# First steps of the second batch: last transposed weights ahead of the softmax, means of w1's last quarter in place of unread products

## The chip, the cores and the metric

The kernel runs on one core of a Trainium2 chip. The time is device microseconds of one execution, the median of several runs. TensorE (PE in the profile), VectorE (DVE), ScalarE (ACT), GpSimd (POOL) and the DMA queues each work through an instruction stream of their own and wait for each other by semaphores.

## The reference

Attention with a threshold is followed by a Fourier mix and a two-layer network, all in float32 (8 batches, 8 heads, 576 rows, 64 columns a head; hidden size 2048):

```python
scores = scale * q @ k.T
thresh = max(scores) - tau                       # along the row
attn = where(scores >= thresh, exp(scores - max(scores)), 0)
attn = attn / (sum(attn) + 1e-9)
x = heads side by side of (attn @ v)             # (8, 576, 512)
mixed = real(fft(fft(x, axis=1), axis=2))
u = x + mixed
un = (u - mean(u)) / sqrt(var(u) + 1e-6)         # along the row
out = u + relu(un @ w_ch1) @ w_ch2
```

The mean of a row is not taken from u. Instead each column of w_ch1 (w1 in the kernel) has its mean over the 512 input rows subtracted once, which gives the same product. For that, TensorE multiplies a quarter of w1 (512 of its 2048 columns) with a matrix of 1/512 ("means of w1"). Two of the four row blocks of w1 are also mirrored by a product with a permutation.

## The kernel before: what the change and the prediction touch

A step `i` is one tile of 128 query rows of one pair of heads; a batch has 20 steps. In a step the scores of the tile are made, then its softmax, and then the transposition of the weights of the step before, `i - 1`. Steps 20 to 39 are `second_batch`. Beside attention it does the Fourier mix of the first batch (`mix`), the last conversions of w_ch2 (`advance`: the input is float64 as integers, made float32 in several passes of VectorE, ScalarE and GpSimd), and the first products of the network (`fill`).

```python
def busy(n):                      # products that nobody reads
    for _ in range(n):
        pd = ps.tile([128, 4, 128], FP32, tag="mm", bufs=4, name="pd")
        nc.tensor.matmul(pd[:, :, :], ones[:, :], four, start=True, stop=True)   # 128x512
...
def column_means(g):              # means of w1's quarter g
    pm = ps.tile([128, 512], FP32, tag="mm", bufs=4, name="pm")
    for c in range(ND):           # 4 row blocks
        nc.tensor.matmul(pm[:, :], ones[:, :], w1[c][:, cols], start=(c == 0), stop=(c == ND - 1))
def mirrored(g):
    for c in (1, 3):
        pr = ps.tile([128, 512], FP32, tag="mm", bufs=4, name="pr")
        nc.tensor.matmul(pr[:, :], mirror[:, :], w1[c][:, cols], start=True, stop=True)
def less_mean(eng, g, c):         # L377
    rows = prs[g][c // 2][:, :] if c % 2 else w1[c][:, cols]
    eng.tensor_tensor(out=w1[c][:, cols], in0=rows, in1=means[g][:, :], op=ALU.subtract)
def copy_mean(g):                 # L1247: ScalarE, out of the product's bank
    nc.scalar.copy(mean[:, :], means[g][:, :])
...
def softmax(i, between=None, meanwhile=None):
    for j in range(nh):           # two heads
        nc.vector.tensor_reduce(out=neg[...], in_=sc[j][...], op=ALU.max, negate=True)   # L461
    meanwhile()                   # here: advance of the step before
    for j in range(nh):
        nc.scalar.activation(out=ej, in_=sc[j][...], func=ACT.Exp, bias=neg[...])        # L469
        ... thr by ScalarE (j == 0, L473)
        nc.vector.scalar_tensor_tensor(out=ej, in0=sc[j][...], scalar=thr[...], in1=ej,
            op0=ALU.is_ge, op1=ALU.mult, accum_out=den[...])                             # L477
    nc.vector.reciprocal(den, den)
    rec = ...                     # a copy by GpSimd (L501)

def weights_in_parts(i):          # transposed_weights(i) runs it to its end
    nc.tensor.transpose(pe[:, 0, :], e[:, 512:640], ident)   # L541
    nc.tensor.transpose(pe[:, 1, :], rec, ident)             # L544
    ... 4 (last tile of a pair) or 8 transposes into pw      # L560
    nc.scalar.copy(...)           # ends, recs (L548, L552), e_t (L562, L564)
def weighted_values(n, part):     # pv: 20 products (L589) of e_t and ends with v, x by VectorE (L597)
...
def first_sums_w1():              # called at the second group of tokens, about 386 us
    for c in range(2):            # L880
        nc.vector.tensor_tensor(out=s_u[c], in0=a_w1[1][0][c], in1=a_w1[1][1][c], op=ALU.add)
    for c in range(2):            # L884
        nc.vector.tensor_tensor(out=a_w1[1][0][c], in0=a_w1[0][0][c], in1=a_w1[1][0][c], op=ALU.subtract)
...
def second_batch(i):
    first = i - per_batch         # 0 to 19
    if first != 1:
        scores(i)
    softmax(i, None, lambda: (advance(first - 1), advance(first - 1)))
    ...
    if first == 0:
        transposed_weights(i - 1)
        weighted_values(n - 1, 1)
        scores(i + 1)
        busy(4)
        ... fold of x by VectorE, start of the mix
        mix(3)
        mix(3)                    # py: products of the mix (L692)
    elif first == 1:
        mix(3)
        transposed_weights(i - 1)
        busy(2)
        mix(2)                    # pa: L709, L713; then tmp (L728, L729) and u_t (L731, L735)
        advance(first)            # L298, L301, L306, L309, L312
        advance(first)
    elif first == 2:
        mix(2)
        transposed_weights(i - 1)
        mix(2)
        column_means(LAST)
        copy_mean(LAST)
        mirrored(LAST)
        for c, eng in ((1, nc.vector), (3, nc.vector), (0, nc.gpsimd), (2, nc.gpsimd)):
            less_mean(eng, LAST, c)
        weighted_values(n, 0)
        advance(first)
        advance(first)
    else:
        fill()                    # ph: hidden products (L822), relu (L827 ScalarE, L829 VectorE)
        transposed_weights(i - 1)
        ...
        if t == 3:
            prep_pair(n + 1)      # pq, pk, pt: q and k of the next pair transposed
```

Products go to PSUM tiles of one pool ("mm", four banks) and free them when their reader is done. The first two batches are written in a fixed order on all engines. From the third on only TensorE's order is fixed, and a scheduler places the other engines' instructions. It may hoist them into the earlier part: `first_sums_w1` is written there, and before the change its two sums L880 run at 170.7 and 172.5 us.

Of the kernel before, what the change touches and what calls it, by code (L numbers as in the profile page):

```python
# [47 lines left out]
def kernel(  # L48
# [12 lines left out]
    nc = tc.nc  # L61
# [43 lines left out]
    def busy(n):  # L105

        for _ in range(n):
            pd = ps.tile([128, 4, 128], FP32, tag="mm", bufs=4, name="pd")
            four = bass.AP(
                tensor=ones.tensor, offset=ones.offset, ap=[list(ones.ap[0]), [0, 4], [1, 128]]  # L110
            )
            nc.tensor.matmul(pd[:, :, :], ones[:, :], four, start=True, stop=True)  # L112
# [244 lines left out]
    def column_means(g):  # L357
        cols = slice(WC * g, WC * (g + 1))
        pm = ps.tile([128, 512], FP32, tag="mm", bufs=4, name="pm")
        for c in range(ND):  # L360
            nc.tensor.matmul(
                pm[:, :], ones[:, :], w1[c][:, cols], start=(c == 0), stop=(c == ND - 1)
            )
        means[g] = pm
# [9 lines left out]
    def less_mean(eng, g, c):  # L374
        cols = slice(WC * g, WC * (g + 1))
        rows = prs[g][c // 2][:, :] if c % 2 else w1[c][:, cols]
        eng.tensor_tensor(out=w1[c][:, cols], in0=rows, in1=means[g][:, :], op=ALU.subtract)  # L377
# [45 lines left out]
    def scores(i):  # L423
        n, t = divmod(i, NT)
        qT, kT = heads[n][0:2]

        nh = 2 if t < 4 else 1
        sc = [ps.tile([128, 2, 512], FP32, tag="sc", name=f"sc{j}") for j in range(nh)]
        if t < 4:
            for c in range(2):  # L430
                for j in range(2):
                    hp = slice(64 * j, 64 * j + 64)
                    nc.tensor.matmul(  # L433
                        sc[j][:, c, 0:HALF], qT[hp, 128 * t : 128 * t + 128],
                        kT[hp, HALF * c : HALF * (c + 1)], start=True, stop=True,
                    )
        else:

            for j, c, c0, k0, w in (
                (0, 0, 0, 0, HALF), (1, 0, 0, 64, HALF), (0, 1, 0, HALF, HALF),  # L440
                (1, 1, 0, 64 + HALF, 512 - HALF), (1, 1, 512 - HALF, 0, 64),
            ):
                hp = slice(64 * j, 64 * j + 64)
                nc.tensor.matmul(  # L444
                    sc[0][hp, c, c0 : c0 + w], qT[hp, 512:S], kT[hp, k0 : k0 + w],
                    start=True, stop=True, skip_group_check=True,
                )
        steps[i] = (sc, nh)

    def softmax(i, between=None, meanwhile=None):  # L450

        t = i % NT
        sc, nh = steps[i]
        neg = sb.tile([128, 2], FP32, tag="neg", bufs=3, name="neg")
        thr = sb.tile([128, 2], FP32, tag="thr", bufs=3, name="thr")
        den = sb.tile([128, 2], FP32, tag="den", bufs=3, name="den")


        e = sb.tile([128, 2 * S], FP32, tag="e", name="e")
        for j in range(nh):  # L460
            nc.vector.tensor_reduce(  # L461
                out=neg[:, j : j + 1], in_=sc[j][:, :, 0:HALF], axis=AXIS_XY, op=ALU.max,
                negate=True,
            )
        if meanwhile is not None:
            meanwhile()
        for j in range(nh):
            ej = e[:, S * j : S * (j + 1)].rearrange("p (c n) -> p c n", c=2)
            nc.scalar.activation(  # L469
                out=ej, in_=sc[j][:, :, 0:HALF], func=ACT.Exp, bias=neg[:, j : j + 1], scale=1.0  # L470
            )
            if j == 0:
                nc.scalar.activation(  # L473
                    out=thr[:, 0:nh], in_=neg[:, 0:nh], func=ACT.Identity,
                    bias=thr_off[:, :], scale=-1.0,
                )
            nc.vector.scalar_tensor_tensor(  # L477
                out=ej, in0=sc[j][:, :, 0:HALF], scalar=thr[:, j : j + 1], in1=ej,
                op0=ALU.is_ge, op1=ALU.mult, accum_out=den[:, j : j + 1],
            )  # L480

            nc.vector.tensor_scalar(
                out=den[:, j : j + 1], in0=den[:, j : j + 1], scalar1=1e-9, scalar2=None,
                op0=ALU.add,
            )
            if between is not None:
                between()
                between = None
        nc.vector.reciprocal(den[:, 0:nh], den[:, 0:nh])  # L489
        rec = None  # L490
        if normalized(i // NT):
            nc.vector.tensor_scalar(  # L492
                out=e[:, 0:S], in0=e[:, 0:S], scalar1=den[:, 0:1], scalar2=None, op0=ALU.mult
            )
            if nh == 2:
                nc.scalar.activation(  # L496
                    out=e[:, S : 2 * S], in_=e[:, S : 2 * S], func=ACT.Copy, scale=den[:, 1:2]
                )
        else:
            rec = sb.tile([128, 2 * D], FP32, tag="rec", name="rec")  # L500
            nc.gpsimd.tensor_copy(  # L501
                rec[:, :].rearrange("p (j d) -> p j d", j=nh), _repeated(den[:, 0:nh], 2 * D // nh)
            )
        if t == 4:
            nc.scalar.copy(e[:, S : S + 64], e[:, 512:S])
        steps[i] = (e, rec)

    def transposed_weights(i):
        for _ in weights_in_parts(i):
            pass  # L510
# [366 lines left out]

    def first_sums_w1():
        for c in range(2):
            nc.vector.tensor_tensor(  # L880
                out=s_u[c], in0=a_w1[1][0][c], in1=a_w1[1][1][c], op=ALU.add
            )
        for c in range(2):
            nc.vector.tensor_tensor(  # L884
                out=a_w1[1][0][c], in0=a_w1[0][0][c], in1=a_w1[1][0][c], op=ALU.subtract
            )
# [358 lines left out]
    def copy_mean(g):  # L1245
        mean = sb.tile([128, WC], FP32, tag="u", bufs=2, name="mean")
        nc.scalar.copy(mean[:, :], means[g][:, :])  # L1247
        means[g] = mean
# [30 lines left out]
    def advance(at):  # L1279
        for run in chunks.get(at, ()):  # L1280
            next(run, None)
# [24 lines left out]
    def mix(count):  # L1306
        nonlocal spent, mixed
        for _ in range(count):
            done = next(mixes[0], None)
            if done is None:  # L1310
                mixes.pop(0)
                mixed += 1
                break
            spent += done

    def second_batch(i):

        nonlocal budget
        n, t = divmod(i, NT)
        first = i - per_batch  # L1320
        if first != 1:
            scores(i)
        softmax(i, None, lambda: (advance(first - 1), advance(first - 1)))
        chunks.pop(first - 1, None)
        transfers(first)
        fold_more()
        if first == 0:
            transposed_weights(i - 1)
            weighted_values(n - 1, 1)
            scores(i + 1)  # L1330
            busy(4)
            folds.append(fold_rows(n - 1))
            while folds:
                fold_more()
            load_v(n + 1)
            start_batch(0)
            mix(3)
            mix(3)
        elif first == 1:
            mix(3)  # L1340
            transposed_weights(i - 1)
            busy(2)
            mix(2)
            advance(first)
            advance(first)
        elif first == 2:
            mix(2)
            transposed_weights(i - 1)
            mix(2)
            column_means(LAST)  # L1350
            copy_mean(LAST)
            mirrored(LAST)
            for c, eng in ((1, nc.vector), (3, nc.vector), (0, nc.gpsimd), (2, nc.gpsimd)):
                less_mean(eng, LAST, c)
            weighted_values(n, 0)
            advance(first)
            advance(first)
        else:
            fill()
# [3 lines that stand above are left out]
            fill()  # L1363
            if t == 3:
                prep_pair(n + 1)
            fill()
            if t == 2:
                weighted_values(n, 0)
            if t == 0:
                weighted_values(n - 1, 1)  # L1370
                folds.append(fold_rows(n - 1))
                load_v(n + 1)
        if first == 16:
            fold_halves(1)
        if first < 3:
            budget += 3 * per_slot
# [94 lines left out]
```

## Time and profile before

| what | value |
|---|---|
| time, median of 3 runs | 1679.7 us (1679.39 to 1679.97) |
| span of the profiled execution | 1678.0 us |
| TensorE, VectorE, ScalarE, GpSimd busy | 97%, 68%, 50%, 35% |
| shares of the chain that ended last | TensorE 76%, VectorE 15%, ScalarE 7% |
| mean granted TensorE clock | 0.996 of full |
| first step of the second batch (its scores) | 130.9 us |
| scores of its fourth step | 170.9 us |

An L with a number is a line of the kernel. A row of a timeline has the start and the length in us, the engine, the line, the output and inputs by the program's names, the shape and the count; in brackets stands how long the engine had been idle and what released it. A matmul in float32 leaves two records, so four products of 128x512 are x8. The chain of waits follows the work that ended last back through what released each step. Ends of matmuls are modelled; starts are better to go by.

### The profile page before, as it was taken

The numbers are of one execution on the slowest core, as the hardware profiler recorded it, in microseconds if no ns is written. First come the engines' busy times: TensorE is split into PE (matmuls) and PEld (weight loads), VectorE is DVE, ScalarE is ACT, GpSimd is POOL, SyncE is SP. The second block draws the span as 40 slices with busy tenths as digits, with TensorE's granted clock in tenths as the row PEclk, the third lists the DMA queues.
The fourth block names the chain that finished last, engine by engine and source line by source line (L and its number), as shares of the span: only waits on it lengthen the run. The fifth ranks groups of instructions, "written<-read, shape, count | busy, mean of one in ns | idle before, by whom it ended". The sixth has DMA issues, their size and how long they took to land.

```text
span 1678.0 us, 28904 instructions
## 1 busy us (share of the span) xinstructions
PE 1626.3 (97%) x10838; PEld 1277.1 (76%) x10838; DVE 1142.1 (68%) x2518; ACT 837.2 (50%) x1817; POOL 581.2 (35%) x779
## 2 busy tenths in 40 slices
PE   8998889999999999999999999999999999999998
PEld 4555555566887788878888778787878788889998
DVE  6885786565857676866576758686686858664454
ACT  5764675543545464545354546455646545432111
POOL 5773463040520433134322143213242144224232
PEclk9999999999999999999999999999999999999999
DMA  5323231010010101000101010110101010000000
GB/s 163 114 55 109 57 87 45 25 35 21 16 37 13 35 16 42 22 28 8 28 16 41 9 35 15 42 22 25 25 16 41 22 28 9 14 1 13 14 13 13
DMA packets 130384, 57.48 MB, mean 34 GB/s; under 512 B 121123, under 2 KB 121125, under 8 KB 130246
## 3 DMA queue, kind: packets, MB, share of 16 engines
q1 hardware_dynamic: 128854, 55.35, 12.3%
q8 instruction: 86, 1.41, 0.4%
q14 instruction: 52, 0.43, 0.1%
q10 hardware_dynamic: 1392, 0.30, 0.1%
HBM read 46.02 MB, written 9.44 MB: 33 GB/s over the span
## 4 chain that ended last, share of the span: by engine, by line
PE 76%; DVE 15%; ACT 7%; issue 2%; POOL 1%; DVEq 0%; ACTq 0%
PE ph L926 24%; PE po L1090 18%; PE pv L589 8%; PE sc L433 7%; PE pw L560 5%; PE po L848 3%; DVE e L477 3%; DVE neg L461 2%; ACT e L469 2%; DVE hs L1051 2%; PE sc L444 2%; PE ph L822 1%; PE py L692 1%; PE pd L112 1%; PE pa L709 1%
## 5 line engine op out<-in xcount | busy, mean ns | idle before, releaser
L469 ACT ACTIVATE e<-sc,neg 128x576 f32<-128x576 f32 x288 | 212.2, 737 | 239.5 <-DVE neg L461 238.9
L461 DVE TENSOR_REDUCE neg<-sc 128x1 f32<-128x576 f32 x288 | 206.2, 750 | 172.7 <-PE sc L433 160.9
L477 DVE SCALAR_TENSOR_TENSOR e<-sc,thr,e 128x576 f32<-128x576 f32 x288 | 229.8, 811 | 56.8 <-ACT thr L473 53.0
L1090 PE MATMUL po<-w,hs 128*128 128x256 f32 x1024 | 246.2, 383 | 0.0
L1090 PEld LDWEIGHTS po<-w,hs 128*128 128x128 f32 x1024 | 186.0, 190 | 32.8 <-issue 11.2
L926 PE MATMUL ph<-u_t,w 128*128 128x128 f32 x1536 | 187.8, 276 | 0.0
L926 PEld LDWEIGHTS ph<-u_t,w 128*128 128x128 f32 x1536 | 179.3, 192 | 4.4 <-issue 3.3
L560 PE MATMUL pw<-ident,e 128*128 128x128 f32 x1152 | 169.9, 274 | 10.5 <-ACT kT L406 2.7
L562 ACT COPY e_t<-pw 128x512 f32<-128x512 f32 x256 | 148.6, 594 | 59.9 <-PE pw L560 59.3
L433 PE MATMUL sc<-kT,qT 64*128 64x288 f32 x1024 | 167.4, 429 | 8.2 <-DVE e L477 7.6
L560 PEld LDWEIGHTS pw<-ident,e 128*128 128x128 f32 x1152 | 134.5, 141 | 29.4 <-issue 4.3
L935 DVE TENSOR_TENSOR hs<-ph,hs 128x512 f32<-128x512 f32 x160 | 107.0, 685 | 72.1 <-PE ph L926 46.8
L433 PEld LDWEIGHTS sc<-kT,qT 64*128 64x128 f32 x1024 | 92.6, 186 | 69.2 <-issue 38.8
L926 PE MATMUL ph<-t_u,s_w 128*128 128x128 f32 x1024 | 126.9, 278 | 2.1 <-POOL t_u L900 1.8
L804 DVE SCALAR_TENSOR_TENSOR u<-po,rstd,u 128x256 f32<-128x256 f32 (+1 forms) x164 | 75.5, 484 | 73.8 <-PE po L1090 71.9
L926 PEld LDWEIGHTS ph<-t_u,s_w 128*128 128x128 f32 x1024 | 120.3, 193 | 5.0 <-issue 2.3
L1090 PE MATMUL po<-hs,s_tile 128*128 128x256 f32 x512 | 122.1, 382 | 0.0
L496 ACT ACTIVATE e<-e,den 128x576 f32<-128x576 f32 x96 | 74.9, 780 | 63.6 <-DVE den L489 62.9
L1090 PEld LDWEIGHTS po<-hs,s_tile 128*128 128x128 f32 x512 | 93.6, 190 | 13.6 <-issue 2.1
L943 ACT ACTIVATE hs<-hs 128x512 f32<-128x512 f32 x112 | 69.3, 630 | 63.4 <-DVE hs L935 63.4
L622 POOL TENSOR_TENSOR half<-x 128x287 f32<-128x287 f32 x48 | 40.2, 857 | 126.5 <-ACT x L595 70.7
L492 DVE TENSOR_SCALAR e<-e,den 128x576 f32<-128x576 f32 x120 | 79.7, 664 | 3.5
(199 smaller groups left out, 2868.9 us busy)
## 6 DMA issues: line engine op xcount, KB each, us to landing
hs<-in_moe_w_ch_dram SPq DMA_DIRECT2D x23, 512.0 KB, 4.4
out_dram<-u SPq DMA_DIRECT2D x36, 256.0 KB, 2.2
qk_in<-in_q_dram SPq DMA_DIRECT2D x64, 128.0 KB, 2.4
v_in<-in_v_dram SPq DMA_DIRECT2D x64, 128.0 KB, 2.4
qk_in<-in_k_dram SPq DMA_DIRECT2D x31, 128.0 KB, 2.4
w<-in_moe_w_ch_dram SPq DMA_DIRECT2D x6, 512.0 KB, 8.3
qk_in<-in_k_dram SPq DMA_DIRECT2D x31, 64.0 KB, 2.3
stage<-in_moe_w_ch_dram SPq DMA_DIRECT2D x3, 512.0 KB, 3.9
```

The costliest lines, as they stand in the source:

```text
L433: nc.tensor.matmul(sc[j][:, c, 0:HALF], qT[hp, 128 * t : 128 * t + 128], kT[hp, HALF * c : HALF * (c + 1)], start=True, stop=True,)
L461: nc.vector.tensor_reduce(out=neg[:, j : j + 1], in_=sc[j][:, :, 0:HALF], axis=AXIS_XY, op=ALU.max, negate=True,)
L469: nc.scalar.activation(out=ej, in_=sc[j][:, :, 0:HALF], func=ACT.Exp, bias=neg[:, j : j + 1], scale=1.0)
L477: nc.vector.scalar_tensor_tensor(out=ej, in0=sc[j][:, :, 0:HALF], scalar=thr[:, j : j + 1], in1=ej, op0=ALU.is_ge, op1=ALU.mult, accum_out ...
L492: nc.vector.tensor_scalar(out=e[:, 0:S], in0=e[:, 0:S], scalar1=den[:, 0:1], scalar2=None, op0=ALU.mult)
L560: nc.tensor.transpose(pw[:, c, :], e[:, c0 : c0 + 128], ident[:, :])
L562: nc.scalar.copy(e_t[:, 4 * j : 4 * j + 4, qs], pw[:, :, :])
L589: nc.tensor.matmul(pv[64 * j : 64 * j + 64, 0:m], vt[:, 2 * c + j, :], e_t[:, 4 * j + c, 0:m] if c < 4 else ends[:, 0:m], start=(c == 0), ...
L804: nc.vector.scalar_tensor_tensor(out=u, in0=product, scalar=self.rstd[:, t : t + 1], in1=u, op0=ALU.mult, op1=ALU.add,)
L926: nc.tensor.matmul(banks[name][:, 128 * q : 128 * q + 128], left[c][:, 512 * part + 128 * q : 512 * part + 128 * q + 128], right[c], start ...
L935: nc.vector.tensor_tensor(out=to, in0=bank, in1=to if other is None else other, op=ALU.add)
L1090: nc.tensor.matmul(bank[:, 0 : DM // 2], left[p], right[p], start=start and p == 0, stop=p == NK - 1, skip_group_check=True,)
```

## The change

In the first step of the second batch (`first == 0`) the transposition of the last weights, with its copies by ScalarE, is written ahead of the softmax. Unread products that only kept TensorE at work (`busy(4)`, `busy(2)`) give way to the means and the mirrored blocks of w1's last quarter, which stood in the third step. The subtractions of the means go to the second step with them. The two sums L880 are kept in their place in the program's order, so that the scheduler no longer hoists them between the subtractions. What is computed stays the same; six unread products are gone.

```diff
     def first_sums_w1():
         for c in range(2):
-            nc.vector.tensor_tensor(
+            tc.keep_in_program_order(nc.vector.tensor_tensor(
                 out=s_u[c], in0=a_w1[1][0][c], in1=a_w1[1][1][c], op=ALU.add
-            )
+            ))
...
             scores(i)
+        if first == 0:
+
+            transposed_weights(i - 1)
         softmax(i, None, lambda: (advance(first - 1), advance(first - 1)))
...
         if first == 0:
-            transposed_weights(i - 1)
             weighted_values(n - 1, 1)
             scores(i + 1)
-            busy(4)
+            column_means(LAST)
+            copy_mean(LAST)
...
             mix(3)
             transposed_weights(i - 1)
-            busy(2)
             mix(2)
+            mirrored(LAST)
+            for c, eng in ((1, nc.vector), (3, nc.vector), (0, nc.gpsimd), (2, nc.gpsimd)):
+                less_mean(eng, LAST, c)
...
             mix(2)
-            column_means(LAST)
-            copy_mean(LAST)
-            mirrored(LAST)
-            for c, eng in ((1, nc.vector), (3, nc.vector), (0, nc.gpsimd), (2, nc.gpsimd)):
-                less_mean(eng, LAST, c)
             weighted_values(n, 0)
```

In the built program TensorE's order is otherwise the same to the end. On VectorE the two sums L880 now stand ahead of the two subtractions L884, where before only L884 stood, and some ten rows around them change places.

## The prediction

> **What bounds the kernel now.** I read the page first: its first two parts say which engine fills the span, and where in it that engine has air.
>
> ```profile
> PE 1626.3 (97%) x10838; PEld 1277.1 (76%) x10838; DVE 1142.1 (68%) x2518; ACT 837.2 (50%) x1817; POOL 581.2 (35%) x779
> PE   8998889999999999999999999999999999999998
> ```
>
> TensorE is busy 97% of 1678.0 us; the air is in the first six slices, about 250 us. The change touches TensorE between 132 and 173 us, so I asked for the busy time of each stretch there, and of a late one for comparison. After the stretch and its length come the busy time (and records) of each engine, the granted TensorE clock, and the DMA share and rate.
>
> ```profile
> 160.00:180.00 20.00, 16.23 (x81) 9.27 (x82) 13.89 (x31) 8.96 (x22) 12.74 (x14) 1.00 0.01 1
> 360.00:400.00 40.00, 40.00 (x269) 29.31 (x266) 28.63 (x66) 20.05 (x45) 7.74 (x14) 1.00 0.12 30
> ```
>
> From 360 us TensorE is full: work moved there is hidden if it is not TensorE's. At 160 us it is not full, so a wait removed there may bring time. The timeline of TensorE (start, length, what; in brackets the idle time before, and its releaser) has the pieces concerned:
>
> ```profile
> 132.30 0.60 PE L560 MATMUL pw<-ident,e 128*128 128x128 f32 x4
> 135.93 4.04 PE L589 MATMUL pv<-e_t,v_in 128*64 128x320 f32 x16 [3.03 <-ACT e_t L564]
> ...
> 163.24 3.70 PE L361 MATMUL pm<-w,ones 128*128 128x512 f32 x8
> 166.78 1.88 PE L371 MATMUL pr<-w,mirror 128*128 128x512 f32 x4
> ...
> 178.11 0.65 PE L398 MATMUL pq<-ident,qk_in 128*128 128x128 f32 x4 [2.10 <-ACT hs L827]
> ```
>
> The product pv waits 3.03 us for ScalarE's copy e_t. ScalarE's timeline says why: the copies stand behind the two exponentials of the next tile, though what they copy was finished at 132.9.
>
> ```profile
> 132.92 0.74 ACT L469 ACTIVATE e<-sc,neg 128x576 f32<-128x576 f32 x1 [1.32 <-DVE neg L461]
> ...
> 134.41 0.41 ACT L552 COPY ends<-pe 64x64 f32<-64x64 f32 x2
> 134.84 0.42 ACT L552 COPY recs<-pe 64x64 f32<-64x64 f32 x2
> 135.29 0.58 ACT L564 COPY e_t<-pw 128x512 f32<-128x512 f32 x1
> ```
>
> After that idle time TensorE's clock drops: single microseconds of the same table give 0.50 until 139.2.
>
> ```profile
> 136.00:137.00 1.00, 1.00 (x4) 0.46 (x6) 0.12 (x1) 0.00 (x0) 0.29 (x1) 0.50 0.66 250
> 138.00:139.00 1.00, 1.00 (x6) 0.47 (x4) 0.00 (x0) 0.00 (x0) 0.00 (x0) 0.50 1.12 397
> ```
>
> Lastly VectorE from 165 to 175 us, where its order holds up the softmax that TensorE waits for at 178.11:
>
> ```profile
> 167.91 0.69 DVE L377 TENSOR_TENSOR w<-pr,mean 128x512 f32<-128x512 f32 x1 [3.09 <-PE pr L371]
> 170.65 1.22 DVE L880 TENSOR_TENSOR s_w<-w,w 128x1024 f32<-128x1024 f32 x1 [2.05 <-POOL w L377]
> 171.79 0.68 DVE L377 TENSOR_TENSOR w<-pr,mean 128x512 f32<-128x512 f32 x1
> 172.51 1.23 DVE L880 TENSOR_TENSOR s_w<-w,w 128x1024 f32<-128x1024 f32 x1
> 173.65 0.42 DVE L597 TENSOR_TENSOR x_first<-pv,recs 128x256 f32<-128x256 f32 x1
> ```
>
> Two waits (3.09 and 2.05 us) and two sums of 1.2 us stand ahead of x_first, and the chain of waits runs through exactly these rows: POOL w L377 to 170.6, s_w, w, s_w, x_first, then L298 and ScalarE to pq.
>
> [...] s_w waits 2.05 us, with a ready subtraction behind it. [...] a second drop (mean clock 0.73 in 234 to 236 us) follows 2.53 us of idle. [...] L298 takes 0.89 us beside a busy GpSimd (156.7) and 0.42 us beside an idle one (174.0).
>
> **The change part by part.** I take the starts of before and carry a shift along the chain; minus is earlier.
>
> 1. *Copies ahead of the exponentials.* TensorE's order here is unchanged; ScalarE's is turned round. The rows pe are done at about 132.45. The four small copies and e_t take 1.37 us in a row (134.51 to 135.88 in the chain), so e_t ends at about 133.9 and pv starts at about 133.95 instead of 135.93: **-2.0**. Idle before it falls from 3.03 to about 1.05 us.
> 2. *The clock.* In before the 20 products of pv take 4.63 us (135.93 to 140.56); the same 20 take about 2.9 us at full clock (192.72 to 195.6, twin of this group). With 1.05 us of idle I expect no drop: **-1.7**. pv then ends at about 136.9. The exponentials now start at 133.9 rather than 132.92, and VectorE's softmax ends at about 137.05 rather than 136.1; that is 0.15 behind pv's end and becomes the limit for x. The shift there is about **-3.55**.
> 3. *Means for busy(4).* Four products of 128x512 replace four of 128x512: 3.58 us (141.60 to 145.3) against 3.54 (163.24 to 166.78). Both lie beside VectorE's fold, whose first result lets py start at 145.44. Zero; the shift stays -3.55. The copy of the mean (0.58) falls into 10.9 us of ScalarE's idle time before 146.77.
> 4. *busy(2) gone, mirrored in.* The first pa starts at 153.93 after 1.79 us of unread products; its inputs are done by 151.9 and the products before it at 152.1. So pa moves by -5.35. The two mirrored products (1.8 us) come behind pa and ahead of the next scores, which move by -3.75. VectorE does two subtractions of 0.65 us more before L298, but pa reached it 1.8 us sooner: L298 moves from 156.82 to about 153.0, **-3.8**. GpSimd's two subtractions (2.5 us) follow four additions that start 5.35 us earlier. They end at about 156.9, where L319 (160.54 before) is due at 156.75: 0.15 lost or nothing.
> 5. *The place they left.* pm and pr took 5.35 us of TensorE (163.24 to 168.59) between the last pa and pv. Now pv follows pa at about 159.45: **-9.2** for pv, the scores after it, and the first hidden product. GpSimd's additions to u_t, which that product's third matmul needs, end near 164.3, when it is due: no loss.
> 6. *VectorE without subtractions and sums.* x_first had waited for all four rows until 173.74. Now it waits only for pv's end, about 161.75, so it starts near 161.85: -11.9. GpSimd is still busy until 164.3, so L298 and L301 may take 1.6 us instead of 0.7, giving back about 1.0. The softmax, ScalarE's relu L827 and pq at 178.11 then move by **-10.9**. The first hidden product ends at about 165.7, so it is not the bound, and the 2.10 us idle ahead of pq nearly closes.
> 7. *The sums later.* In the built order they stand beside the two subtractions L884, which ran at 386.1 to 388.6. They need 2 x 1.2 us of VectorE, in a stretch where TensorE has no idle time. The softmax's den and normalization move back by about 3.2 us. The weights they feed would be ready at about 394.6, and TensorE asks at 395.94: no loss, at most +0.5.
>
> From 180 us on the order is the same on all engines but for this spot, and transfers are issued relative to the computation. The shift should reach the end whole: -10.9 and up to +0.5. I take -10.6: 1679.7 - 10.6 = 1669.1.
>
> **The rivals.**
> (a) *The clock stays half speed behind pv.* [...] Against: 1.69 us before 161.58 and 2.10 us before 178.11 drew no drop in the trace. It would leave -9, 1670.5.
> (b) *GpSimd becomes the bound.* Its additions to u_t, the subtractions of w1 and the conversion stand in one queue from 151 to 164 us, and the hidden product waits for the last of them. If GpSimd runs 2 us later than I have it, the hidden product and ScalarE's relu follow: -9, 1670.7. For it: my two figures meet at 164.3 without slack. Against: VectorE's softmax is about 1.2 us behind anyway.
> (c) *The early gain is swallowed later.* From 360 us TensorE is full, and full TensorE absorbs nothing: work only starts sooner. A transfer could catch it, but the seven weight transfers issued at 134 to 138 us are on the way until about 147, and the first use moves to 153. I give it little. It would make 1674 to 1679.
> (d) *Fewer unread products cool the clock elsewhere*[...]: 1.6 us either way.
>
> **Range and chances.** -10.6 is the sum; (a) and (b) each cost about 2, (d) is plus or minus 1.6, and part 6 may bring 1 more[...]. So 1666 to 1673 in 8 of 10 cases. Faster by 2% would need 33.6 us, three times all that is at stake: 0.005. Slower by 2% would need something broken in the later schedule: 0.01.
>
> **What would show it.** Right: pv starts near 134 with about 1 us of idle, its 20 products take about 2.9 us at clock 1.00, pa starts near 148.6, the second scores after it near 161.8, and pq near 167.2. Wrong: a clock of 0.50 anywhere from 134 to 168; TensorE idle ahead of the first hidden product with a GpSimd u_t row as releaser (b); new idle time of TensorE from 386 to 400 us (part 7); or a shift that is -10 at 180 us and smaller at 400 (c).

## The result and the profile after

The changed kernel takes 1668.51 us (median of 4 runs, 1668.08 to 1671.41) against 1679.55 us: ratio 0.9938, 95% interval 0.9921 to 0.9955. A second series gave 1668.99 us and 0.9936 (0.9923 to 0.9948). That is 11 us, 0.6%.

The profiled execution was the slowest of the four (1671.41 us); its span is 1669.6 us. Up to the first step's scores it runs 1.36 us later than the profile of before, because TensorE's clock fell once more, for 3.41 us from 17.9 us on. I therefore measure each kernel from its own first scores of the second batch (130.86 us in before, 132.22 here).

The page shows the engine lines hardly changed; TensorE's busy time fell by 4.5 us, and one of the first slices is a tenth fuller.

```profile
PE 1621.8 (97%) x10826; PEld 1273.6 (76%) x10826; DVE 1146.0 (69%) x2518; ACT 837.9 (50%) x1817; POOL 581.9 (35%) x779
PE   8998899999999999999999999999999999999998
```

TensorE's timeline of the changed kernel, the pieces that answer to those of before (start, length, what; in brackets the idle time before and its releaser):

```profile
133.66 0.60 PE L560 MATMUL pw<-ident,e 128*128 128x128 f32 x4
135.40 2.37 PE L589 MATMUL pv<-e_t,v_in 128*64 128x320 f32 x16 [1.14 <-ACT e_t L564]
...
151.74 1.88 PE L371 MATMUL pr<-w,mirror 128*128 128x512 f32 x4
...
164.12 1.56 PE L822 MATMUL ph<-u_t,w 128*128 128x384 f32 x4
167.35 1.56 PE L822 MATMUL ph<-u_t,w 128*128 128x384 f32 x4 [1.67 <-POOL u_t L735]
...
169.84 0.60 PE L398 MATMUL pq<-ident,qk_in 128*128 128x128 f32 x4
```

The wait ahead of pv is 1.14 instead of 3.03 us, and its first 16 records take 2.37 instead of 4.04 us. (A product leaves two records: what the prediction calls the 20 products of pv are 10 products in 20 records.) The 2.10 us ahead of pq are gone. In their place stands a new wait: the hidden product ph stops in its middle for 1.67 us, for GpSimd's last row of u_t. Single stretches of the table of busy times have the clock under pv at 1.00:

```profile
134.00:136.00 2.00, 0.86 (x9) 0.38 (x9) 0.91 (x2) 1.93 (x7) 0.00 (x0) 1.00 0.27 60
136.00:138.00 2.00, 2.00 (x18) 0.99 (x14) 1.69 (x5) 0.80 (x2) 0.00 (x0) 1.00 0.56 108
```

ScalarE's copies now stand ahead of the exponential:

```profile
133.86 0.42 ACT L552 COPY ends<-pe 64x64 f32<-64x64 f32 x2 [0.90 <-PE pe L544]
...
134.76 0.59 ACT L564 COPY e_t<-pw 128x512 f32<-128x512 f32 x1
135.24 0.75 ACT L469 ACTIVATE e<-sc,neg 128x576 f32<-128x576 f32 x1
```

VectorE's timeline, where x_first now waits for nothing but pv:

```profile
152.80 0.69 DVE L377 TENSOR_TENSOR w<-pr,mean 128x512 f32<-128x512 f32 x1
153.66 0.69 DVE L377 TENSOR_TENSOR w<-pr,mean 128x512 f32<-128x512 f32 x1 [0.17 <-PE pr L371]
...
157.13 1.66 DVE L314 SCALAR_TENSOR_TENSOR w<-hs,w 128x512 f32<-128x512 uint32 x1
...
163.14 0.42 DVE L597 TENSOR_TENSOR x_first<-pv,recs 128x256 f32<-128x256 f32 x1 [0.74 <-PE pv L589]
```

One row is to be kept in mind: L314 took 1.66 us. The same row of before took 0.68 us. In the changed kernel GpSimd's two subtractions stand beside it. VectorE's timeline of before, then GpSimd's of the changed kernel:

```profile
159.72 0.68 DVE L314 SCALAR_TENSOR_TENSOR w<-hs,w 128x512 f32<-128x512 uint32 x1
```

```profile
155.55 2.69 POOL L377 TENSOR_TENSOR w<-w,mean 128x512 f32<-128x512 f32 x2
158.93 1.27 POOL L319 TENSOR_TENSOR w<-w,hs 128x512 f32<-128x512 f32 x1 [0.69 <-ACT tmp L724]
...
163.66 0.88 POOL L731 TENSOR_TENSOR u_t<-x,tmp 1x289 f32<-1x289 f32 x1
...
166.08 1.22 POOL L735 TENSOR_TENSOR u_t<-x,tmp 1x287 f32<-1x287 f32 x1
```

L314 ends at 158.79 us, 0.55 us after the second subtraction (158.24).

**Where the gain arises, and that it stays.** The table has, for each kernel, how much sooner the scores of the second to fifth step start than in before, each counted from the first step's scores (starts in TensorE's timeline; before: 9.57, 24.96, 40.04 and 51.32 us after them). The runs below are in it too.

| kernel | 2nd | 3rd | 4th | 5th | median us | ratio (95%) |
|---|---|---|---|---|---|---|
| predicted | -3.55 | -3.75 | -9.2 | -10.9 | 1669.1 | |
| changed, first profile | -3.55 | -3.63 | -9.31 | -9.91 | 1668.51 | 0.9938 (0.9921 to 0.9955) |
| changed, again | -3.55 | -3.62 | -9.30 | -9.91 | 1668.99 | 0.9936 (0.9923 to 0.9948) |
| copies first alone | -3.54 | -3.61 | -3.60 | -3.55 | 1676.74 | 0.9982 (0.9975 to 0.9989) |
| idle filled | -1.65 | -1.65 | -1.67 | -0.33 | 1679.23 | 0.9997 (0.9989 to 1.0005) |
| sums kept alone | +0.04 | +0.05 | +0.05 | -2.48 | 1675.93 | 0.9975 (0.9967 to 0.9984) |
| means alone | -0.34 | -0.34 | -0.38 | -2.09 | 1676.80 | 0.9985 (0.9978 to 0.9991) |
| changed, copies late | +0.03 | +0.04 | -5.64 | -6.24 | 1672.75 | 0.9961 (0.9948 to 0.9973) |
| changed, sums hoisted | -3.54 | -3.61 | -3.85 | -6.01 | 1672.90 | 0.9957 (0.9944 to 0.9971) |
| changed, busy(2) back | -3.54 | -1.89 | -7.55 | -8.17 | 1673.41 | 0.9962 (0.9949 to 0.9974) |
| GpSimd later | -3.55 | -3.61 | -9.29 | -10.21 | 1669.85 | 0.9944 (0.9930 to 0.9957) |
| GpSimd later, row on VectorE | -3.55 | -3.62 | -9.29 | -8.74 | 1672.03 | 0.9957 (0.9944 to 0.9969) |
| subtractions early on VectorE | -3.54 | -3.61 | -9.30 | -10.91 | 1668.25 | 0.9931 (0.9919 to 0.9944) |
| subtractions early on GpSimd | -3.55 | -3.61 | -9.29 | -11.17 | 1670.40 | 0.9938 (0.9925 to 0.9950) |

From 253 us on the two profiles run in step for nearly 400 us. In absolute times the changed kernel is ahead by 8.55 us at the fifth scores and by a constant 8.66 from 253 to 631 us of before's profile (1.36 more each, without the late start). Nothing is lost at 386 us, where the sums now stand. Between 632 and 640 us it loses 1.15 us: TensorE there waits for VectorE, as it did not before. TensorE's timeline of the changed kernel, first profile:

```profile
624.57 1.99 PE L1090 MATMUL po<-w,hs 128*128 128x256 f32 x8 [0.54 <-DVE u L804]
627.16 0.66 PE L560 MATMUL pw<-ident,e 128*128 128x128 f32 x4 [0.48 <-DVE qT L399]
```

The same rows of before have no idle time. Both profiles of the changed kernel have these two waits; what makes VectorE late there was not tested. All the other kernels of the table have one or both of them too: 0.40 us with the sums kept alone, 1.64 us with the idle time filled, where hardly any shift is left. So the loss cannot be put down to the change. It comes back at 757 us, where the same idle time of 1.81 us lets the clock fall in the profile of before but not in that of the changed kernel. That it comes back is chance: other executions have this fall or lack it. First before, then the changed kernel, seven products (14 records) each:

```profile
756.69 2.97 PE L926 MATMUL ph<-t_u,s_w 128*128 128x128 f32 x14 [1.81 <-POOL t_u L900]
```

```profile
749.19 1.83 PE L926 MATMUL ph<-t_u,s_w 128*128 128x128 f32 x14 [1.81 <-POOL t_u L900]
```

From 767 us on it is 8.73 us ahead, at 1407 us 8.77, and from 1485 us to the last products 8.41 (9.77 without the late start): near 1470 us a wait of TensorE grew from 0.31 to 0.66 us. So nearly all of the gain reaches the end.

Medians (4 to 21 runs) scatter by about 1 us and more, because a fall of the clock costs up to 1.7 us (4.04 against 2.37 us for the first 16 records of pv) and the falls lie differently in each execution. Differences of 1 us are therefore read from the shifts, and larger ones from the times. The mean granted clock of each run tells how many falls it had, by an estimate: one fall, 3.41 us at half clock in some 1670 us, lowers the mean by 0.001. The runs of before have 0.9961 on average (55 runs), nearly 4 falls; those of the changed kernel 0.9983 and 0.9984 (4 and 5 runs), 1.6 to 1.7 falls.

**The changed kernel again,** beside three of the experiments below (copies late, GpSimd later, row on VectorE):

> The changed kernel itself, beside the next three on one chip: 1668.5 to 1669.5, and from the second step's scores to the fifth's the same 9.9 us gained as in its first profile.

Measured: 1668.99 us, and the shifts of its second profile agree with those of the first to 0.01 us at every step. A shift is thus a far sharper measure than a time.

### The profile page after: what moved, and what is told of

Same layout as the page of the kernel before. It is cut to its first block, busy times and chain, and to the rows that moved or that the text cites. A ratio compares the mean times of both kernels' runs of the same rounds, so it can differ in the third digit from the quotient of the medians.

```text
span 1669.6 us, 28885 instructions
## 1 busy us (share of the span) xinstructions
PE 1621.8 (97%) x10826; PEld 1273.6 (76%) x10826; DVE 1146.0 (69%) x2518; ACT 837.9 (50%) x1817; POOL 581.9 (35%) x779
## 4 chain that ended last, share of the span: by engine, by line
PE 76%; DVE 15%; ACT 7%; issue 2%; POOL 1%; DVEq 0%; ACTq 0%; POOLq 0%
PE ph L926 23%; PE po L1090 18%; PE pv L589 8%; PE sc L433 7%; PE pw L560 5%; PE po L848 3%; DVE e L477 3%; DVE neg L461 2%; ACT e L469 2%; DVE hs L1051 2%; PE sc L444 2%; PE ph L822 1%; PE py L692 1%; PE pa L709 1%; PE pn L782 1%
## 5 line engine op out<-in xcount | busy, mean ns | idle before, releaser
L461 DVE TENSOR_REDUCE neg<-sc 128x1 f32<-128x576 f32 x288 | 206.2, 750 | 171.4 <-PE sc L433 158.5
L1086 POOL TENSOR_TENSOR hs<-hs,s_tile 128x512 f32<-128x512 f32 x32 | 42.3, 1323 | 117.5 <-PE po L1090 113.8
```

The lines of the kernel that those rows point to most:

```text
L461: nc.vector.tensor_reduce(out=neg[:, j : j + 1], in_=sc[j][:, :, 0:HALF], axis=AXIS_XY, op=ALU.max, negate=True,)
```

## The experiments

**Copies first alone.** On the kernel before:

```diff
             scores(i)
+        if first == 0:
+            transposed_weights(i - 1)
         softmax(i, None, ...)
...
         if first == 0:
-            transposed_weights(i - 1)
             weighted_values(n - 1, 1)
```

> Only the copies of the last transposed weights go ahead of the softmax; unread products, means and sums stay as before. My theory (parts 1 and 2 of the prediction): pv starts 2.0 us sooner and runs at full clock, so the scores after it come 3.55 us sooner and the whole rest moves by that: 1676.0. Rival: the clock drops all the same, and only the wait is saved: 1677.6. Rival: VectorE's later softmax takes the place of the wait: under 1 us, about 1679.

Measured: 1676.74 us and -3.54 us at the second scores, which stays to the end. The part does alone what it does in the whole. TensorE's timeline has the wait at 1.14 us and pv at full speed:

```profile
134.28 2.38 PE L589 MATMUL pv<-e_t,v_in 128*64 128x320 f32 x16 [1.14 <-ACT e_t L564]
```

**Idle filled.** How much of the 3.54 us is the clock? Here the wait stays and unread work is put into it:

```diff
             transposed_weights(i - 1)
+            busy(2)
             weighted_values(n - 1, 1)
```

> The kernel before with two more unread products of 128x512 (1.8 us) in the 3.03 us in which TensorE waits for the copy e_t; no wait is taken away. If the idle time is what halves the clock under pv, pv's 20 products take 2.9 us instead of 4.6 and the time falls by 1.7 us to 1677.9, by adding work. If the clock is halved by something else (the weight transfers that run at the same time), pv stays at 4.6 us and the time at 1679.6.

Measured: pv takes 2.38 us again, and the second scores come 1.65 us sooner, with more work and the same wait. So the idle time causes the half clock, not the weight transfers: they ran at the same time (379 GB/s in 136 to 138 us). Chance does not explain the fall under pv either: all four profiles with the wait of 3.03 us have it (before, sums kept alone, means alone, copies late), and none of the ten with a wait of 1.13 to 1.32 us. But the time fell by no more than its scatter, to 1679.23 us. TensorE's timeline and the table of busy times show where the profiled execution lost the gain again.

```profile
132.23 1.88 PE L112 MATMUL pd<-ones 128*128 128x512 f32 x4
135.43 2.38 PE L589 MATMUL pv<-e_t,v_in 128*64 128x320 f32 x16 [1.32 <-ACT e_t L564]
...
175.96 1.09 PE L398 MATMUL pq<-ident,qk_in 128*128 128x128 f32 x4 [2.12 <-ACT hs L827]
```

```profile
176.00:178.00 2.00, 2.00 (x10) 2.00 (x11) 1.93 (x7) 1.59 (x5) 1.72 (x2) 0.50 0.00 0
```

The 2.12 us of idle time ahead of pq brought the clock down in this execution, and 1.34 of the 1.65 us were lost again. In the profile of before 2.10 us at the same place had not. A further 1.8 us went at 632 to 636 us, in the waits named above, and 1.2 us came back at 757 us. Why the one gap drew a fall and the other did not was not shown; the gain is only sure where the gap itself goes.

**Sums kept alone.** On the kernel before:

```diff
-            nc.vector.tensor_tensor(
+            tc.keep_in_program_order(nc.vector.tensor_tensor(
                 out=s_u[c], in0=a_w1[1][0][c], in1=a_w1[1][1][c], op=ALU.add
-            )
+            ))
```

> Only the two sums L880 are kept in their place in the program's order (they go to about 386 us); all else as before. My theory: x_first then waits only for pv's end (171.0) and runs at about 171.1 instead of 173.65, the softmax behind it comes 2.5 us sooner, pq 2.1 and the rest 2.3 us: 1677.3. Nothing is lost at 386 us. Rival: VectorE's 2.4 us come back at 386 us, where TensorE is full: about 1679.6. Rival: the last subtraction is bound by GpSimd anyway: under 0.5 us.

Measured: -2.48 us at the fifth scores, and none of it comes back at 386 us. The median is 4 us lower; in the profile a fall of the clock near 235 us is missing too (-1.6 us). It is not this execution alone: the 13 runs have a mean clock of 0.9969 against 0.9961, about 0.8 falls fewer by the estimate above. Why is open. VectorE's timeline has x_first right behind pv:

```profile
168.14 1.48 DVE L377 TENSOR_TENSOR w<-pr,mean 128x512 f32<-128x512 f32 x2 [3.08 <-PE pr L371]
171.25 0.42 DVE L597 TENSOR_TENSOR x_first<-pv,recs 128x256 f32<-128x256 f32 x1 [1.63 <-PE pv L589]
```

**Means alone.** The means, mirrored blocks and subtractions move as in the change, and both calls of busy go; the copies stay behind the softmax, and the sums are left to the scheduler:

```diff
-            busy(4)
+            column_means(LAST)
+            copy_mean(LAST)
...
-            busy(2)
             mix(2)
+            mirrored(LAST)
+            ... less_mean, all four
```

> Only the means and mirrored blocks move into the place of the unread products; copies behind the softmax and sums left to the scheduler, which now puts one sum ahead of the third step's maxima (L461), where it waits for GpSimd's two subtractions. If removing unread products counts by itself, 5.35 us of TensorE are saved: 1674.2. My theory: the scores of the fourth step come sooner by no more than 2 to 3 us, since VectorE waits some 3.5 us for GpSimd in the sum: 1677.

Measured: the fourth scores come only 0.38 us sooner, though 5.4 us of TensorE's work between the last pa and pv are gone. The fifth come 2.09 us sooner. The scheduler hoists the sums all the same, to where GpSimd's subtractions have not been done:

```profile
161.78 1.23 DVE L880 TENSOR_TENSOR s_w<-w,w 128x1024 f32<-128x1024 f32 x1 [2.40 <-POOL w L377]
162.92 1.42 DVE L461 TENSOR_REDUCE neg<-sc 128x1 f32<-128x576 f32 x2
```

The softmax's maxima stand behind a sum that waits 2.40 us and takes 1.2 us. (The 0.34 us at the second scores are what the clock would give, by an estimate, if the fall began 0.7 us ahead of pv here: in before it began just with it, at 135.92 and 135.93 us, and 0.7 us less of half clock under pv are 0.35 us.)

**Changed, copies late; changed, sums hoisted.** The changed kernel with one part undone each: `transposed_weights(i - 1)` back behind the softmax, or the sums without `keep_in_program_order`.

> The changed kernel with the last transposed weights put back behind the softmax, all else kept. By the theory the wait of 3.0 us and the half clock under pv come back: the second scores 3.55 us later, 1672.1. If the copies' place is worth something only beside the unread products, less than 2 us: 1670.

> The changed kernel with the two sums L880 left to the scheduler again, which now puts one ahead of the third step's maxima. By the run with the means alone, VectorE waits there for GpSimd's two subtractions, some 3.5 us, and the softmax behind it is late: the time rises by 4.4 us over the changed kernel, 1673. If the sums matter only by their own 2.4 us, it rises by 2.4: 1671.

Measured: without the copies' place the second scores lose 3.58 us, and the time is 1672.75 us; the part is worth the same in company as alone. TensorE's timeline has the wait and the slow products back:

```profile
135.91 4.07 PE L589 MATMUL pv<-e_t,v_in 128*64 128x320 f32 x16 [3.03 <-ACT e_t L564]
```

Without the kept sums the fifth scores lose 3.90 us (-6.01 for -9.91), and the time is 1672.9 us. They are worth 2.5 us on the kernel before, but 3.9 beside the moved means: moving the means needs the sums to be held. TensorE's timeline of the run with hoisted sums shows the price:

```profile
160.09 1.11 PE L560 MATMUL pw<-ident,e 128*128 128x128 f32 x4 [4.52 <-ACT tmp L724]
```

In the table of busy times the clock is at 0.50 from about 158.2 to 165.0 us, in this wait and behind it: twice the 3.41 us of each fall in before.

**Changed, busy(2) back.**

```diff
             transposed_weights(i - 1)
+            busy(2)
             mix(2)
             mirrored(LAST)
```

> The changed kernel with the two unread products put back ahead of pa. If they are on the path, as part 4 has it, pa and all behind it come 1.8 us later: 1670.4. If they kept the clock up, the time falls, or stays.

Measured: the third scores lose 1.73 us, the fifth 1.74: the two unread products were on the path and no help to the clock here. The time rises by more than that, from 1668.99 to 1673.41 us. Of these 4.4 us 0.7 lie between the two series: before took 1679.68 us in the one and 1680.40 in the other. In this run's profile the clock also falls near 750 us, behind 1.83 us of idle time (the seven products above take 3.22 us instead of 1.83), which costs 1.4 us. The five runs have a mean clock of 0.9968 against 0.9984, about 1.6 falls more by the estimate; why they have more is not settled.

**GpSimd later; and a row on VectorE.** These ask where 1.0 of the predicted 10.9 us stayed. In the changed kernel L314 takes 1.66 instead of 0.68 us beside GpSimd's subtractions, and L319 starts 0.8 us later than predicted behind it.

```diff
             mirrored(LAST)
-            for c, eng in ((1, nc.vector), (3, nc.vector), (0, nc.gpsimd), (2, nc.gpsimd)):
-                less_mean(eng, LAST, c)
+            for c in (1, 3):
+                less_mean(nc.vector, LAST, c)
...
             transposed_weights(i - 1)
             mix(2)
+            for c in (0, 2):
+                less_mean(nc.gpsimd, LAST, c)
```

The second run also gives one of the two single-row additions of this batch (L731 and L735 on one partition) to VectorE.

> The changed kernel with GpSimd's two subtractions of the mean left in the third step, behind the additions to u_t, as before. My theory of the missing 0.9 us: [...] L319 and all of GpSimd's queue behind it run 1 us late and the hidden product ph waits for u_t. Then L314 is back at 0.7 us, ph waits 0.6 instead of 1.7 us, and the rest moves by -1.0 against the changed kernel: 1667.7. Rival: L319 waits for ScalarE, not for L314, and L314 is slow because of L319 of the chunk before: no difference. Rival: GpSimd's subtractions, now later, delay the next conversion by 1.7 us and with it the softmax: slower by up to 1 us.

> As the run with GpSimd's subtractions later, and of the four additions of a single row to u_t at the end of GpSimd's queue two go to VectorE, which is idle for 0.74 us there. If GpSimd's queue is the bound of ph, another 1.8 us leave it: ph waits for nothing and the rest moves by -1.7 against the changed kernel, where ScalarE's softmax becomes the bound: 1666.9. If the softmax is the bound already, the two additions delay it on VectorE by 0.2 to 0.9 us: no gain over the run without them, or a loss.

Measured, later alone: L314 is back at 0.68 us and ph waits 0.16 instead of 1.67 us (0.6 expected). Yet the fifth scores gain only 0.3 of the 1.0 us expected, and pq waits 0.76 us for ScalarE's relu. TensorE's, VectorE's and GpSimd's timelines of this run:

```profile
164.46 1.56 PE L822 MATMUL ph<-u_t,w 128*128 128x384 f32 x4 [0.16 <-POOL u_t L735]
...
167.87 0.66 PE L398 MATMUL pq<-ident,qk_in 128*128 128x128 f32 x4 [0.76 <-ACT hs L827]
```

```profile
155.75 0.68 DVE L314 SCALAR_TENSOR_TENSOR w<-hs,w 128x512 f32<-128x512 uint32 x1
...
162.10 1.10 DVE L298 TENSOR_SCALAR w<-hs 128x512 int32<-128x512 int32 x1
163.13 1.56 DVE L301 TENSOR_SCALAR hs<-hs 128x512 int32<-128x512 int32 x1
164.62 1.41 DVE L461 TENSOR_REDUCE neg<-sc 128x1 f32<-128x576 f32 x2
165.95 1.66 DVE L314 SCALAR_TENSOR_TENSOR w<-hs,w 128x512 f32<-128x512 uint32 x1
```

```profile
164.37 2.68 POOL L377 TENSOR_TENSOR w<-w,mean 128x512 f32<-128x512 f32 x2
```

The next conversion pays: L298 and L301 take 2.7 us instead of 1.4 beside GpSimd's rows. The subtractions took their collision with them: the next L314 takes 1.66 us, and it ends 0.56 us after the second subtraction (167.61 and 167.05). The second rival of the expectation came true in part. With the row on VectorE, ph no longer waits, but the two single-row operations take 1.04 and 1.58 us there, pq waits 2.65 us, and the fifth scores are 1.2 us worse than in the changed kernel: the softmax was the bound as soon as GpSimd was not. The time, 1672.03 us, is 3.0 us above the changed kernel's second series, of which the shift accounts for 1.2; its runs have a mean clock of 0.9966 against 0.9984, about 1.8 falls more by the estimate, and why is not settled.

**Subtractions early, on VectorE or on GpSimd.** The two row blocks that GpSimd subtracts need only the mean and are not mirrored, so they may be done a step sooner:

```diff
# on VectorE                                  # or on GpSimd
             transposed_weights(i - 1)
+            for c in (0, 2):
+                less_mean(nc.vector, LAST, c)
             mix(2)
...
             copy_mean(LAST)
+            for c in (0, 2):                 # second run only
+                less_mean(nc.gpsimd, LAST, c)
```

> The changed kernel with GpSimd's two subtractions on VectorE, in its 2.29 us of idle time ahead of the second step's tmp, so that GpSimd has 2.7 us less to do and no subtraction stands beside L314 or the next conversion. [...] the shift at the fifth scores becomes -10.7 to -11 (now -9.9): 1668. If the next conversion is slowed by the additions to u_t all the same, it stays at -10.2, as in the run with the subtractions later.

> The changed kernel with GpSimd's two subtractions directly behind the copy of the mean, where GpSimd is idle for 11 us. They run beside VectorE's fold (L673, L682), on which py waits[...]. The gain in the third step is that of the run on VectorE; in sum 0.2 to 1 us better than the changed kernel, about 1668.2. [...]

Measured: -10.91 and -11.17 us at the fifth scores, the predicted amount. L314 takes 0.68 us in both, and ph waits 0.66 and 0.39 us. VectorE's and TensorE's timelines of the run with the subtractions on VectorE:

```profile
155.07 0.68 DVE L314 SCALAR_TENSOR_TENSOR w<-hs,w 128x512 f32<-128x512 uint32 x1
```

```profile
164.28 1.56 PE L822 MATMUL ph<-u_t,w 128*128 128x384 f32 x4 [0.66 <-POOL u_t L735]
```

In the run on GpSimd it was GpSimd that gave way (3.24 us for the two subtractions instead of 2.69), while VectorE's fold kept its 0.97 us:

```profile
143.95 3.24 POOL L377 TENSOR_TENSOR w<-w,mean 128x512 f32<-128x512 f32 x2 [5.03 <-ACT mean L1247]
```

Both versions gain 1.0 to 1.3 us on the changed kernel by the shifts, and it stays: from the first scores to the end the profiles are 10.8 us ahead of before, those of the changed kernel 9.8 and 9.7. By their times (1668.25 and 1670.40 us) they cannot be told from it; the first has the lowest ratio of all, 0.9931 (0.9919 to 0.9944). Their runs have mean clocks of 0.9974 and 0.9968, so more falls than those of the changed kernel.

## Why the prediction was right, point by point

The predicted 1669.1 us and the measured 1668.5 lie 0.6 us apart, and most steps were met singly. That the sum came so close is partly luck, as the end of this part shows.

- *Part 1, the copies:* the wait fell from 3.03 to 1.14 us (1.05 predicted). Shown by the run with the copies alone and by the one with them undone.
- *Part 2, the clock:* 1.65 us by the run with filled idle time (1.7 predicted). That VectorE's softmax would be the next limit, and the shift 3.55 instead of 3.7, held to 0.01 us.
- *Part 3, means for busy(4):* nothing, as said: copies alone and the changed kernel have the same second scores.
- *Part 4, busy(2) and mirrored:* pa moved by 5.4 us (149.70 less 1.36 against 153.76), and the third scores by 3.63 (3.75 predicted; its own terms, -5.35 and +1.8, add up to -3.55). Putting busy(2) back cost 1.7 us.
- *Part 5:* the fourth scores moved by 9.31 us (9.2 predicted). To the 5.35 us of products came 0.3 us from the wait for tmp, which fell from 1.69 to 1.37 us.
- *Part 6 was too large by 1.0 us:* -9.9 at the fifth scores where -10.9 was predicted. The step that failed is the one before it, in parts 4 and 5: that GpSimd would reach L319 with "0.15 lost or nothing", and end its additions near 164.3 "when it is due". That assumed L314 at 0.68 us. It took 1.66, because GpSimd's subtractions stood beside it, so L319 started 0.8 us late (158.93 less 1.36 is 157.57). GpSimd's queue ended 1.6 us late (167.3 less 1.36 is 165.9): its four rows of one partition took 3.64 us beside VectorE's next conversion, 2.72 in before. So the first hidden product was the bound, which part 6 had ruled out. VectorE itself was early enough: it gave back 0.6 us where 1.0 was allowed, and its maxima L461 came 11.3 us sooner (164.74 less 1.36 against 174.66). This is rival (b), which I had named with a loss of 2 us, by way of a queue that is too long. The missing 1.0 us is the collision with L314: the same subtractions done a step sooner, on either engine, give L314 back its 0.68 us and the whole 10.9 us, while a shorter wait of ph remains; done later they meet the next L314, and only 0.3 us come back.
- *Part 7, the sums later:* no loss at 386 us. VectorE's timeline of the changed kernel has them at 378.35, and TensorE has no idle time from 360 to 400 us:

```profile
378.35 2.35 DVE L880 TENSOR_TENSOR s_w<-w,w 128x1024 f32<-128x1024 f32 x2
380.62 2.35 DVE L884 TENSOR_TENSOR w<-w 128x1024 f32<-128x1024 f32 x2
```

- *Rival (a)* did not come, but my argument against it was weak: idle gaps of 1.69 and 2.10 us drew no fall in one trace, and 2.12 us did in another. *Rival (c)* did not come where I looked for it: the shift is rigid to 631 us. But 1.15 us went at 632 to 640 us and 0.3 near 1470 us, and without the fall of before at 757 us the first would have stayed lost. *Rival (d)* is visible as scatter: the profile of before has falls at 115, 136, 235 and 757 us, that of the changed kernel at 18, 110 and 226 us.

The median gained 11.0 us, the profiles 9.9 by shift and 9.8 to the end, where the sum of the prediction was 10.6. The rest of about 1 us is of the size of one fall. The profile of the changed kernel had three falls, its runs only 1.6 to 1.7 on average; of before both had about four. So the runs avoid about two falls, one of them under pv. The other was forecast only as the 1.6 us either way of rival (d), and it made up for what the collision cost: that is luck. Why it is avoided was not tested.

The prediction allowed for slower rows of VectorE beside a busy GpSimd at L298 and L301 alone (0.89 and 0.91 us in before, where each takes 0.42 us beside an idle GpSimd). L314 was slowed as well: it took 0.68 us alone and 1.66 beside a subtraction of GpSimd.

## What to carry to other kernels

Look for a copy that stands behind a wait it does not need (here pv waited 3.03 us instead of 1.14), and for an operation that a scheduler hoisted to a place where its inputs are late (s_w waited 2.05 us with a ready subtraction behind it). Each such row costs its wait, and with it perhaps a fall of TensorE's clock (1.65 us under pv). Where TensorE was not full, such time came back here and nearly all of it stayed; unread products belong only into idle time, never ahead of ready work (they gained 1.65 us in the one place and cost 1.7 us in the other). Before moving work to an idle engine, see what stands beside it on VectorE and GpSimd at that time: the collision that made L314 take 1.66 instead of 0.68 us moved along with the work, to the next L314.

## What I had not expected of the hardware

Each fall of the clock in the profiles of before and of the changed kernel lasts 3.41 us; the one behind the wait of 4.52 us with hoisted sums lasts twice that (158.2 to 165.0 us). Within each of these two profiles the falls lie whole multiples of 3.413 us apart: those of before at 115.4, 135.9 and 234.9 us by 6 and 29 of them, those of the changed kernel at 17.9, 110.1 and 226.1 us by 27 and 34. The two profiles do not line up: from the start of the span the falls of before lie 2.80 us past a multiple, those of the changed kernel 0.82 us. A gap shorter than a fall can be enough, and its length alone does not decide: gaps of 2.12 and 2.53 us had a fall in some executions, 2.10 us had none in another, nor had 2.51 us ahead of 228.8 us with the copies late, and 1.81 us drew a fall at 757 us in before and none at the same rows of the changed kernel. The busy share alone does not decide either: the fall at 17.9 us of the changed kernel followed 3.42 us in which TensorE was busy for 2.34, and with the copies late none followed the stretch from 224.85 to 228.26 us, in which it was busy for 1.44. One collision cost VectorE 1.0 us on an operation of 0.68 us, while in another placing GpSimd gave way (3.24 us for two subtractions instead of 2.69). In both it was the engine that began second: L314 at 157.13 us after a subtraction at 157.0, and GpSimd's subtraction at 143.95 after the fold's L673 at 143.48.
